# Weight preparation cut into paced steps, and routing steps moved, in a fused attention, mixture-of-experts and bilinear kernel

## The chip, the core and the metric

The kernel runs on one core of a Trainium2 chip. Five engines take part, each working through its own instructions in their order: TensorE (PE, with weight loads listed apart as PEld), VectorE (DVE), ScalarE (ACT), GpSimd (POOL), and SyncE (SP), which issues nearly all DMA. They meet only at semaphores. The metric is the device time of one execution in microseconds, taken as the median of several runs; lower is better.

## The reference

Three stages follow one another on 2304 tokens (4 sequences of 576) of width 512.

```python
# 1. linear attention, 8 heads of 64; phi gives 2 x 128 features
q_p, k_p = phi(q), phi(k)
kv  = einsum('bhsf,bhsd->bhfd', k_p, v);  z = k_p.sum(axis=2)
num = einsum('bhsf,bhfd->bhsd', q_p, kv)
den = einsum('bhsf,bhf->bhs', q_p, z)[..., None] + 1e-06
x = num / den                                  # becomes 2304 x 512
# 2. mixture of experts, 8 experts, one expert per token
logits = x @ w_gate + modality_bias[modality_id]
e_idx = argmax(logits, 1); gate_w = softmax(logits)[row, e_idx]
out[mask] = gate_w[mask, None] * (relu(x[mask] @ w1[e]) @ w2[e])     # 512 -> 1024 -> 512
# 3. bilinear layer, d_ff = 1536
return (out @ w_a) * (out @ w_b) @ w_out
```

All inputs of the first two stages are float32. The three weights of stage 3 arrive as float64 (8 bytes a number) and are narrowed to float32 on the chip.

## The kernel before

**Numbers in two parts.** Most matmuls of stages 2 and 3 work on operands that are split into a rounded high part and the remainder, and make three products (helper lines L54, L55, L56: high by high, low by high, high by low). ACT casts the high part and DVE subtracts to get the low one. Such pairs are `wh`/`wl` (expert weights, L552/L553), `mxh`/`mxl` (gathered tokens, L576/L577), `hh`/`hl` (the hidden layer, ACT L591 and DVE L592) and `yh`/`yl` (the input of stage 3, L747/L748, with differences `ysum` made first at L762).

**Attention** runs in rounds over units of two heads or so: `pjp` projections (PE) to `m` and `df` (DVE) to `kp` (ACT), then `kxp` (PE), its copy `kx` (DVE, L217), `qtp` transposes (PE) copied to `qts` (ACT, L190), `nmp` (PE), and `rec` and `x` (DVE). PE's order there is the order in which the code issues. Tokens are treated in two halves of 1152; each half has a route.

**Routing** of a half turns its logits into an expert and a place for each token: a gate (`lg`, `mx`, `gt`), a rank, a place (`vals`, `col`, `pl`) and a table. The table is two lookups by one-hot matmuls: `tbp` gives `idx`, the tokens of each tile, and `tbq` gives `perm` and `g2`, for the way back. The first half's steps are handed to attention's rounds 4, 5 and 7 and have a lower priority; the second half's go to slots of the expert stage.

**The expert stage** has 4 tiles of tokens and 8 slots per tile. A slot is 48 matmuls. In slots 0 to 3 the loop `l1` makes two of the eight blocks of the hidden layer: PE fills `hp`, ACT makes `hh`, DVE makes `hl`, and two blocks are under way at most before PE needs the first one's buffer back. In slots 4 to 7 `l2` makes one of four output blocks in two groups of columns; ACT copies each group from `yp` to `y` (L604). At the start of a slot the code runs that slot's entries of a table `side`, then splits the weights of two slots on, and in slots 4 to 6 transposes the next tile's gathered tokens (`mxt`, L573).

**Weight preparation for stage 3** is such side work. The 1536 columns are 12 blocks `f`; ten are prepared during the expert stage, two in stage 3. For each half block `narrow` fetches the raw 8-byte numbers (SP, L688, 768 KB), ACT takes the absolute value (`cvs`, L692), POOL clamps from below (L693), and DVE builds the float32 numbers (L694, L696, L698, L699, L701). After both halves DVE forms sums of the parts (L710 to L713, each 128x256), ACT and DVE split the result (`whi`, L718; `wsum`, L719) in two ranges of 1024 and 1280 columns, and SP stores both parts to a scratch `wsc` (L720, L721). In stage 3 `fw` is loaded from there (L730).

**Order.** Instructions of each engine are put in order by a planner that follows priorities and its own estimates of time. The ten preparations are given a priority lower by 200 than the rest, each as one block of work issued at a slot spread from 3 to 28 of 32. At slot 28 `open_first` closes the preparation's buffers, opens the pools of stage 3 in the same place (so that `ysum` may lie where a `wsum` was), issues the first loads of `fw`, and prepares the first tokens of stage 3 (`first`: two differences, five casts `yh`, five remainders `yl`), at the low priority too.

**The branch.** After the last slot stands `If(nts > NTMIN)` (L983): more tiles only for an uneven routing. It is not taken with these inputs. In the program, PE's first matmul behind it waits for ACT's and DVE's counts that cover everything ahead of the branch on these two engines.

**Stage 3** makes 504 groups of `abp` from `yh`/`yl` and `fw`, multiplies, and multiplies by the third weight; results leave by an indirect DMA of POOL.

Of the kernel before, what the change touches and what calls it, by code (L numbers as in the profile page):

```python
# [20 lines left out]
P = 128  # L21
# [37 lines left out]
class Attn:  # L59
    def __init__(self, nc, tc, ctx, cst, qk, v, vt, xs, lgp):  # L60
        self.nc, self.tc = nc, tc
        self.qk, self.v, self.vt, self.xs = qk, v, vt, xs
        self.cst, self.lgp = cst, lgp
        pool = lambda n, b, **kw: ctx.enter_context(tc.tile_pool(name=n, bufs=b, **kw))
        self.p_ld = pool("a_ld", 2, side="right")
        self.p_df = pool("a_df", 5, side="right")
        self.p_v = pool("a_v", 3)
        self.p_x = pool("a_x", 2)
        self.p_sm = pool("a_sm", 4)
        self.p_kx = pool("a_kx", 2)  # L70
# [130 lines left out]
    def kx(self, u, b):  # L201
# [11 lines left out]
        x = st["kx", b] = self.p_kx.tile([P, 2, 2, 73], F32, tag=f"kx{b}", name="kx")  # L213
        if u == 1 and not b:
            self.first = nc.vector.tensor_copy(x, ps).ins
        else:
            nc.vector.tensor_copy(x, ps)  # L217

    def num(self, u, *parts):
# [4 lines left out]
        for b, h in parts:  # L224
            qt = st.pop(("qt", b, h))
            for j in range(4 if b < 2 else 2):
                for c in range(2):
                    for m in range(2):
                        mm = slice(64 * m, 64 * m + 64)
                        kx = st["kx", b if b < 2 else m][:, c, h if b < 2 else j, :]  # L230
                        nc.tensor.matmul(ps[mm, o, :], qt[:, c, j, mm], kx, start=c == 0, stop=c == 1)
# [102 lines left out]
class Route:  # L334
# [4 lines left out]
    def steps(self, wk, ps, tag, after=None):  # L339
# [7 lines left out]
        return [start, self.rank, self.place, self.table]  # L347
# [4 lines left out]
    def gate(self):  # L352
# [10 lines left out]
        for m in range(2):  # L363
# [3 lines left out]
            nc.vector.tensor_add(lg, lg if m else self.lgp, tmp)  # L367
        mx = self.w([NG], "mx")
        nc.vector.tensor_reduce(out=mx, in_=lg, op=ALU.max, axis=AX.X)
        nc.vector.tensor_sub(lg, lg, mx.unsqueeze(2).to_broadcast([P, NG, E]))  # L370
        ex = self.w([NG, E], "ex")
# [24 lines left out]
    def place(self):  # L396
# [12 lines left out]
        sel = self.w([NG, E], "sel")  # L409
        vals = self.w([3, NG], "vals")  # L410
        for i, src in enumerate((R[:, :NG, :], pf[:, 0, :].unsqueeze(1).to_broadcast([P, NG, E]),
                                 pf[:, 1, :].unsqueeze(1).to_broadcast([P, NG, E]))):
            nc.vector.tensor_mul(sel, oh[:, :NG, :], src)
            nc.vector.tensor_reduce(out=vals[:, i, :], in_=sel, op=ALU.add, axis=AX.X)
        r, te, of = vals[:, 0, :], vals[:, 1, :], vals[:, 2, :]

        def floordiv(val, steps, name):
            k = steps.shape[1]
            t = self.w([NG, k], name + "c")
            nc.vector.tensor_tensor(out=t, in0=val.unsqueeze(2).to_broadcast([P, NG, k]),  # L420
                                    in1=steps.unsqueeze(1).to_broadcast([P, NG, k]), op=ALU.is_ge)
            q = self.w([NG], name + "q")
            nc.vector.tensor_reduce(out=q, in_=t, op=ALU.add, axis=AX.X)
            return q

        def rest(val, q, step, name):
            t = self.w([NG], name)
            nc.vector.scalar_tensor_tensor(out=t, in0=q, scalar=-float(step), in1=val, op0=ALU.mult, op1=ALU.add)
            return t

        jt = floordiv(r, c["kts"][:, 1:KMAX], "jt")
        rc = rest(r, jt, TS, "rc")
        jb = floordiv(rc, c["kp"][:, 1:NSUB], "jb")
        self.pl = rest(rc, jb, P, "pl")
        col = self.col = self.w([NG], "col")
        nc.vector.tensor_add(col, te, jt)
        nc.vector.scalar_tensor_tensor(out=col, in0=col, scalar=float(NSUB), in1=jb, op0=ALU.mult, op1=ALU.add)
        pc = self.w([NG], "pc")
        nc.vector.tensor_add(pc, of, r)
        self.cq = floordiv(pc, c["kp"][:, 1:NG], "cq")  # L440
        self.cl = rest(pc, self.cq, P, "cl")
# [23 lines left out]

    def table(self):
        nc, c = self.nc, self.cst
        NC = NTMAX * NSUB
# [7 lines left out]

        def onehot(out, i, v, n):
            if not self.bp:
                for g in range(NG):
                    nc.gpsimd.tensor_scalar(out=out[:, g, :], in0=c[i][:, :n], scalar1=v[:, g:g + 1], scalar2=None,  # L480
                                            op0=ALU.is_equal)
                return
            nc.vector.tensor_tensor(out=out, in0=c[i][:, :n].unsqueeze(1).to_broadcast([P, NG, n]),
                                    in1=v.unsqueeze(2).to_broadcast([P, NG, n]), op=ALU.is_equal)

        def lookup(name, col, n, row, parts):
            k = len(parts)
            hot = self.w([NG, n], name + "h", BF16)
            rhs = self.w([NG, k, n], name + "r", BF16)
            lhs = self.w([NG, P], "lhs" if self.bp else name + "l", BF16)  # L490
            onehot(hot, "icol", col, n)
            for i, v in enumerate(parts):
                (nc.vector if self.bp else nc.gpsimd).tensor_mul(rhs[:, :, i, :], hot, v.unsqueeze(2).to_broadcast([P, NG, n]))
            onehot(lhs, "i128", row, P)
            ps = self.ps.tile([P, 512], F32, tag=self.tag, name=name)
            for g in range(NG):
                nc.tensor.matmul(ps[:, :k * n], lhs[:, g, :], rhs[:, g].rearrange("p a n -> p (a n)"),
                                 start=g == 0, stop=g == NG - 1)
            return [ps[:, i * n:(i + 1) * n] for i in range(k)]

        def token(out, hi, lo, base):
            t = self.w([NC], "tk")[:, :hi.shape[1]]
            nc.vector.tensor_scalar(out=t, in0=hi, scalar1=float(1 << TB), scalar2=float(base), op0=ALU.mult, op1=ALU.add)
            nc.vector.tensor_add(out, t, lo)

        toks = [c["tokp"][:, i, :] for i in range(2)]
        self.idx = self.pool.tile([P, NC], I32, name=f"idx{self.bp}")
        self.g2 = self.pool.tile([P, NG], F32, name=f"g2{self.bp}")
        self.perm = self.pool.tile([P, NG], I32, name=f"perm{self.bp}")
        hi, lo = lookup("tbp", self.col, NC, self.pl, toks)  # L510
        token(self.idx, hi, lo, 0)
        hi, lo, *gs = lookup("tbq", self.cq, NG, self.cl, toks + [gp[:, i, :] for i in range(3)])
        token(self.perm, hi, lo, HALF * self.bp)
# [6 lines left out]
class Moe:  # L520
# [26 lines left out]
    def splitw(self, T, j):  # L547
# [5 lines left out]
        nc.vector.tensor_sub(lo, src, f32(hi))  # L553
# [25 lines left out]
    def l1(self, T, f):  # L579
# [11 lines left out]
        nc.scalar.activation(hh, ps[:, :, :CG], AF.Relu)  # L591
        nc.vector.scalar_tensor_tensor(out=hl, in0=ps[:, :, :CG], scalar=0.0, in1=f32(hh), op0=ALU.max,  # L592
                                       op1=ALU.subtract)
        T["h", f] = (hh, hl)

    def l2(self, T, m):
        nc = self.nc
        wh, wl = T["w", 4 + m]
        for g in range(2):
# [57 lines left out]
class Moe2:  # L657
# [14 lines left out]
    def pools(self, ctx, ps_a, ps_l):  # L672
# [3 lines left out]
        self.p_t[1] = pool("f_t1", 4)  # L676
# [4 lines left out]
    def narrow(self, pool, f, half, dst, nt):  # L681
        nc = self.nc
        n = 768
        if not self.f64:
            nc.sync.dma_start(out=dst, in_=self.w[f][:, n * half:n * half + n])
            return
        raw = pool.tile([P, n, 2], I32, tag="raw", name="raw", bufs=2)
        nc.sync.dma_start(out=raw.rearrange("p n w -> p (n w)"), in_=self.w[f][:, 2 * n * half:2 * n * half + 2 * n])  # L688
        lo, hi = raw[:, :, 0], raw[:, :, 1]
        t = pool.tile([P, n], I32, tag="t", name="cvt", bufs=nt)  # L690
        s = pool.tile([P, n], I32, tag="s", name="cvs", bufs=nt)
        nc.scalar.activation(s.bitcast(F32), hi.bitcast(F32), AF.Abs)  # L692
        nc.gpsimd.tensor_scalar(out=s.bitcast(F32), in0=s.bitcast(F32), scalar1=LEAST, scalar2=None, op0=ALU.max)  # L693
# [9 lines left out]
    def prep(self, f, pool, nw, nt):  # L703
        nc = self.nc
        w = pool.tile([P, 2304], F32, tag="w", name="wsum", bufs=nw)
        for half, c in enumerate((0, 1280)):
            self.narrow(pool, f, half, w[:, c:c + 768], nt)
# [6 lines left out]
        for x, y in self.CUTS:  # L714
# [6 lines left out]
            nc.sync.dma_start(out=self.wsc[f][1][:, x:y], in_=src)  # L721

# [169 lines left out]
def trn_kernel(ctx, tc, qk, v, vt, w_phi, mod_id, w_gate, bias, wm, wf, out):  # L892
# [10 lines left out]
    with ExitStack() as actx:  # L903
# [13 lines left out]
        for r in range(9):  # L917
            if r + 1 < 8:
                at.load(r + 1)
            if r == 2:  # L920
                bs = bias_load(nc, cpool, keep, bias, mod_id)
                routes = [Route(tc, rpool, lgp[i], bs[i], i) for i in range(2)]
                rsteps = [low(tc, st) for st in routes[0].steps(wkpool, at.ps_c, "c", at.first)]
# [3 lines left out]
            at.round(r, {4: {2: rsteps[:1]}, 5: {2: rsteps[1:3]}, 7: {0: rsteps[3:]}}.get(r, {}) if r > 2 else {})  # L927
            if r == 8:
                order.close()
    with ExitStack() as mctx:  # L930
# [24 lines left out]
        side = {k: [low(tc, rs[f])] for f, k in enumerate((0, 2, 4, 8))}  # L955
# [99 lines left out]
```

## Time and profile before

| | us |
|---|---|
| median of 3 runs (lowest, highest) | 829.94 (828.87, 830.32) |
| the profiled execution, its own time | 837.45 |
| its span, first to last instruction | 835.7 |
| attention, to the first expert matmul | about 176 |
| expert stage, to its last matmul | 176 to 409 |
| stage 3 | 410 to 836 |

The mean granted TensorE clock in the profiled execution is 0.991 of full speed. In the rows further down, a row of a timeline is: start in us, duration in us, engine and line, operation, output and inputs, shape, and in square brackets the idle time that the engine had just before and what released it. A row of waits is: engine, output and line waited for by it, the releaser, then total us, times, longest us. A row of windows is: the stretch in us, its length, then busy us and instruction counts of PE, PEld, DVE, ACT, POOL, then the granted clock, the DMA share and GB/s. A release by `ACTq L983` means the branch at line 983 on ACT's sequencer.

### The profile page before, as it was taken

The numbers are of one execution on the slowest core, as the hardware profiler recorded it, in microseconds if no ns is written. First come the engines' busy times: TensorE is split into PE (matmuls) and PEld (weight loads), VectorE is DVE, ScalarE is ACT, GpSimd is POOL, SyncE is SP. The second block draws the span as 40 slices with busy tenths as digits, with TensorE's granted clock in tenths as the row PEclk, the third lists the DMA queues.
The fourth block names the chain that finished last, engine by engine and source line by source line (L and its number), as shares of the span: only waits on it lengthen the run. The fifth ranks groups of instructions, "written<-read, shape, count | busy, mean of one in ns | idle before, by whom it ended". The sixth has DMA issues, their size and how long they took to land.

```text
span 835.7 us, 18329 instructions
## 1 busy us (share of the span) xinstructions
PE 804.0 (96%) x7283; PEld 755.5 (90%) x7284; DVE 595.1 (71%) x1071; ACT 373.8 (45%) x665; POOL 140.4 (17%) x164
## 2 busy tenths in 40 slices
PE   8999999889999999979999999999999999999996
PEld 6999888789999999979999899999999999999995
DVE  5888898589998999987488854775544676445553
ACT  3656555344544455453345433553333364333332
POOL 1000009342217433310021100030000002000002
PEclk9999999999999999999999999999999999999998
DMA  7666432466768888776499776576666568665632
GB/s 272 193 183 195 149 120 82 115 206 225 249 238 300 289 302 296 271 240 266 170 360 339 254 281 207 187 271 226 205 206 201 186 223 280 206 198 189 224 123 92
DMA packets 85163, 184.22 MB, mean 220 GB/s; under 512 B 27760, under 2 KB 37520, under 8 KB 85072
## 3 DMA queue, kind: packets, MB, share of 16 engines
q1 hardware_dynamic: 81872, 173.21, 61.4%
q0 software_dynamic: 3040, 9.72, 3.4%
q8 instruction: 58, 0.95, 0.5%
q14 instruction: 33, 0.27, 0.1%
q10 hardware_dynamic: 160, 0.07, 0.0%
HBM read 145.21 MB, written 37.75 MB: 219 GB/s over the span
## 4 chain that ended last, share of the span: by engine, by line
issue 44%; PE 4%; POOL 3%; POOLq 0%; ACT 0%
POOL out L800 2%; PE abp L54 1%; PE abp L56 1%; PE abp L55 1%; POOL cvs L693 1%; PE op L55 0%; PE op L54 0%; PE op L56 0%; POOLq L1052 0%; ACT cvs L692 0%; POOLq L800 0%; ACT pc L844 0%
## 5 line engine op out<-in xcount | busy, mean ns | idle before, releaser
L844 ACT COPY pc<-abp 128x384 f32<-128x384 f32 x252 | 120.6, 479 | 199.6 <-PE abp L56 195.9
L54 PE MATMUL abp<-yh,fw 128*128 128x384 f32 x504 | 170.1, 337 | 2.4 <-ACT pc L844 1.3
L56 PE MATMUL abp<-yh,fw 128*128 128x384 f32 x504 | 170.0, 337 | 0.0
L55 PE MATMUL abp<-yl,fw 128*128 128x384 f32 x504 | 169.8, 337 | 0.0
L54 PEld LDWEIGHTS abp<-yh,fw 128*128 128x128 f32 x504 | 94.6, 188 | 11.6 <-ACT pc L844 2.4
L55 PEld LDWEIGHTS abp<-yl,fw 128*128 128x128 f32 x504 | 94.7, 188 | 7.4
L693 POOL TENSOR_SCALAR cvs<-cvs 128x768 f32<-128x768 f32 x24 | 61.5, 2562 | 198.1 <-ACT cvs L692 184.4
L56 PEld LDWEIGHTS abp<-yh,fw 128*128 128x128 f32 x504 | 94.6, 188 | 0.0
L54 PE MATMUL hp<-mxh,wh 128*128 128x304 f32 x256 | 79.1, 309 | 7.9 <-DVE hl L592 6.8
L55 PE MATMUL op<-fw,gh 128*128 128x512 f32 x216 | 85.7, 397 | 0.0
L54 PE MATMUL op<-fw,gh 128*128 128x512 f32 x216 | 85.1, 394 | 0.0
L56 PE MATMUL op<-fw,gl 128*128 128x512 f32 x216 | 85.0, 394 | 0.0
L55 PE MATMUL yp<-hl,wh 128*128 128x304 f32 x256 | 77.3, 302 | 1.7 <-DVE hl L592 1.7
L55 PE MATMUL hp<-mxl,wh 128*128 128x304 f32 x256 | 78.2, 306 | 0.0
L56 PE MATMUL hp<-mxh,wl 128*128 128x304 f32 x256 | 77.8, 305 | 0.0
L56 PE MATMUL yp<-hh,wl 128*128 128x304 f32 x256 | 77.8, 304 | 0.0
L54 PE MATMUL yp<-hh,wh 128*128 128x304 f32 x256 | 76.9, 302 | 0.0
L800 POOL DMA_INDIRECT out<-o,perm x18 | 18.3, 1019 | 348.3 <-ACT o L799 341.2
L190 ACT ACTIVATE qts<-qtp 128x512 f32<-128x512 f32 (+1 forms) x80 | 38.3, 558 | 64.8 <-PE qtp L187 64.8
L855 DVE TENSOR_TENSOR d<-u,pc 128x768 f32<-128x768 f32 x36 | 34.5, 957 | 32.2 <-ACT pc L844 32.0
L54 PEld LDWEIGHTS hp<-mxh,wh 128*128 128x128 f32 x256 | 48.7, 190 | 9.4 <-issue 6.4
L156 DVE TENSOR_REDUCE m<-pjp 128x8 f32<-128x1024 f32 (+2 forms) x49 | 45.1, 933 | 12.0 <-PE pjp L154 12.0
(191 smaller groups left out, 1587.5 us busy)
## 6 DMA issues: line engine op xcount, KB each, us to landing
fw<-wsc SPq DMA_DIRECT2D x72, 512.0 KB, 5.4
fw<-wsc SPq DMA_DIRECT2D x144, 256.0 KB, 3.3
raw<-in_moe_w SPq DMA_DIRECT2D x24, 768.0 KB, 7.2
s<-in_moe_w SPq DMA_DIRECT2D x32, 512.0 KB, 4.2
fw<-wsc SPq DMA_DIRECT2D x72, 128.0 KB, 5.7
wsc<-whi SPq DMA_DIRECT2D x12, 640.0 KB, 4.3
wsc<-wsum SPq DMA_DIRECT2D x12, 640.0 KB, 6.8
wsc<-whi SPq DMA_DIRECT2D x12, 512.0 KB, 7.0
```

The lines of the kernel that those rows point to most:

```text
L54: nc.tensor.matmul(out, lh, rh, start=start, stop=False)
L55: nc.tensor.matmul(out, lh, rl, start=False, stop=False)
L56: return nc.tensor.matmul(out, ll, rh, start=False, stop=stop).ins
L156: nc.vector.tensor_reduce(out=mv, in_=pv, op=ALU.max, axis=AX.X, apply_absolute_value=True)
L190: nc.scalar.activation(t[:, s, :n, :], ps[:, :n, :], AF.Exp, scale=1.0 - 2.0 * s)
L693: nc.gpsimd.tensor_scalar(out=s.bitcast(F32), in0=s.bitcast(F32), scalar1=LEAST, scalar2=None, op0=ALU.max)
L800: st = nc.gpsimd.indirect_dma_start(out=self.out[:, :], out_offset=bass.IndirectOffsetOnAxis(ap=self.routes[bp].perm[:, c:c + 1], axis=0), ...
L844: copied = nc.scalar.copy(x, ps).ins
L855: nc.vector.tensor_add(d, u, x.unsqueeze(1).to_broadcast([P, 2, n]))
```

## The change

There are five parts.

1. Two pools of attention, `a_df` and `a_ld`, change places, so that the expert stage's buffers lie over other tiles of attention.
2. Routing is cut into seven steps instead of four: the gate into start and score, the place into place and bounds, the table into `table` (`tbp`) and `back` (`tbq`, `perm`, `g2`). The first half's steps go to rounds 4, 5, 5, 6, 7 and 8; the second half's to slots 0, 0, 2, 4, 4, 8, 8.
3. The transposes of the first expert tile from the third on, and the second weight split, are issued only behind the last copy of `kx` (and from the fourth on behind the last `nmp` matmul).
4. A preparation is cut into fetch, clamp (ACT and POOL) and narrow (DVE, with sums and stores in the second half). The 20 half blocks get slots of their own from 2 on; fetch, clamp and narrow of one go to slots k, k+1 and k+2, each issued only behind the latest `hh`/`y` instruction of ACT and the latest `wl`/`hl` instruction of DVE. Three raw buffers instead of two.
5. In stage 3 the last two preparations are cut in the same way, and one pool of `y` tiles has 3 buffers instead of 4.

```diff
+        self.p_df = pool("a_df", 5, side="right")
         self.p_ld = pool("a_ld", 2, side="right")
-        self.p_df = pool("a_df", 5, side="right")
...
-        return [start, self.rank, self.place, self.table]
+        return [start, self.score, self.rank, self.place, self.bounds, self.table, self.back]
...
+    def run(self, tiles, side={}, at=None):
...
+        behind = lambda i, on: self.tc.issue_after(i) if at and on else nullcontext()
         split(0)
         for j in range(NSUB):
-            self.transp(Ts[0], j)
+            with behind(at and at.copied, j > 1), behind(at and at.last, j > 2):
+                self.transp(Ts[0], j)
...
-        split(1)
+        with behind(at and at.copied, True):
+            split(1)
...
-        self.p_t[1] = pool("f_t1", 4)
+        self.p_t[1] = pool("f_t1", 3)
...
+    def jobs(self, f, pool, nw, nraw, ns):
+        st = {}
+
+        def fetch(half):
+            st["raw", half] = self.fetch(f, half, pool, nraw)
+
+        def clamp(half):
+            st["s", half] = self.clamp(st["raw", half], pool, ns)
+
+        def narrow(half):
+            if not half:
+                st["w"] = self.sumw(pool, nw)
+            self.narrow(f, half, st["raw", half], st["s", half], pool, st["w"])
+            if half:
+                self.park(f, st["w"], pool)
+
+        return fetch, clamp, narrow
...
-                rsteps = [low(tc, st) for st in routes[0].steps(wkpool, at.ps_c, "c", at.first)]
+                rsteps = routes[0].steps(wkpool, at.ps_c, "c", at.first)
+                rsteps = [low(tc, st) for st in rsteps[:6] + [lambda: routes[0].back(at.ps_q, "q")]]
...
-            at.round(r, {4: {2: rsteps[:1]}, 5: {2: rsteps[1:3]}, 7: {0: rsteps[3:]}}.get(r, {}) if r > 2 else {})
+            at.round(r, {4: {2: rsteps[:1]}, 5: {0: rsteps[1:2], 2: rsteps[2:4]}, 6: {2: rsteps[4:5]}, 7: {0: rsteps[5:6]},
+                         8: {0: rsteps[6:]}}.get(r, {}) if r > 2 else {})
...
-        def conv(f):
-            with tc.high_priority(offset=-LOWP):
-                m2.prep(f, cv[0], 2, 2)
-
-        K0, K1 = 3, len(tiles) * mo.NJ - 4
+        def conv(f, half, job):
+            def run():
+                with tc.high_priority(offset=-LOWP), tc.issue_after(mo.act), tc.issue_after(mo.dve):
+                    job(half)
+            return run
+
+        K0, K1 = 2, len(tiles) * mo.NJ - 4
         for f in range(NPRE):
-            side.setdefault(K0 + (K1 - K0) * f // NPRE, []).append(lambda f=f: conv(f))
+            fetch, clamp, narrow = m2.jobs(f, cv[0], 2, 3, 2)
+            for half in range(2):
+                k = K0 + (K1 - 2 - K0) * (2 * f + half) // (2 * NPRE)
+                for i, job in enumerate((fetch, clamp, narrow)):
+                    side.setdefault(k + i, []).append(conv(f, half, job))
```

How it moves instructions is seen at three places. In the changed kernel the lines have other numbers (`hl` L603, `wl` L564, `cvt` L720 and L722, `cvs` L724 and L725, `wsum` L727 and L745, sums L736 to L739, `whi` L744, `y` L615, `yh` L791, `yl` L792, `ysum` L806).

First, VectorE at the end of attention, before: the rows of the two lookups (`tk`, `idx0` from `tbp`; `tk`, `perm0`, `g20` from `tbq`) and the next unit's `m`.

```order
L504 TENSOR_TENSOR idx0_2633<-tk_2669,tbp_2659 128x45
L503 TENSOR_SCALAR tk_2708<-tbq_2698 128x9
L504 TENSOR_TENSOR perm0_2635<-tk_2708,tbq_2698 128x9
L514 COPY g20_2634<-tbq_2698 128x9
L515 TENSOR_TENSOR g20_2634<-g20_2634,tbq_2698 128x9
L516 TENSOR_TENSOR g20_2634<-g20_2634,tbq_2698 128x9
L517 TENSOR_TENSOR g20_2634<-g20_2634 128x9
L156 TENSOR_REDUCE m_2715<-pjp_2717 128x8
```

Now, on the same engine, the place where `tbq` is read, at the start of the expert stage.

```order
L588 TENSOR_TENSOR mxl_3144<-mxt_3159,mxh_3143 128x4x128
L564 TENSOR_TENSOR wl_3181<-s_3135,wh_3180 128x1024
L502 TENSOR_SCALAR tk_2978<-tbq_2968 128x9
L316 TENSOR_TENSOR m8_3202<-w8_3190 128x64
L319 TENSOR_SCALAR ltri_3204<-i128_3186,part_3200 128x128
L329 TENSOR_SCALAR tokp0_3214<-tok_3208 128x9
L329 TENSOR_SCALAR tokp1_3217<-tok_3208 128x9
L237 TENSOR_SCALAR rec_3002<-nmp_2985 128x4
L503 TENSOR_TENSOR perm0_2941<-tk_2978,tbq_2968 128x9
L525 COPY g20_2940<-tbq_2968 128x9
```

The second lookup's work has moved by two rounds, behind the third `mxl`, between the constants of the second route and the last `rec` and `x`.

Second, VectorE in the first slots of the last expert tile, before: from the third block's `hl` (`hl_5546`) to the next two.

```order
L592 SCALAR_TENSOR_TENSOR hl_5546<-hp_5520,hh_5545 128x608
L699 SCALAR_TENSOR_TENSOR cvs_5481<-raw_5478,cvs_5481 128x768
L713 TENSOR_TENSOR wsum_5318<-wsum_5318 128x256
L694 TENSOR_SCALAR cvt_5491<-cvs_5492 128x768
L701 TENSOR_TENSOR wsum_5477<-cvt_5480,cvs_5481 128x768
L719 TENSOR_TENSOR wsum_5318<-wsum_5318,whi_5345 128x1024
L553 TENSOR_TENSOR wl_5579<-s_5417,wh_5578 128x1024
L696 SCALAR_TENSOR_TENSOR cvt_5491<-raw_5489,cvt_5491 128x768
L592 SCALAR_TENSOR_TENSOR hl_5575<-hp_5549,hh_5574 128x608
L592 SCALAR_TENSOR_TENSOR hl_5610<-hp_5584,hh_5609 128x608
```

Now, from the third block's `hl` (`hl_5530`) to the next two.

```order
L603 SCALAR_TENSOR_TENSOR hl_5530<-hp_5504,hh_5529 128x608
L737 TENSOR_TENSOR wsum_5079<-wsum_5079 128x256
L738 TENSOR_TENSOR wsum_5079<-wsum_5079 128x256
L722 SCALAR_TENSOR_TENSOR cvt_5330<-raw_5158,cvt_5330 128x768
L739 TENSOR_TENSOR wsum_5079<-wsum_5079 128x256
L724 TENSOR_SCALAR cvs_5252<-cvt_5330 128x768
L745 TENSOR_TENSOR wsum_5079<-wsum_5079,whi_5242 128x1024
L725 SCALAR_TENSOR_TENSOR cvs_5252<-raw_5158,cvs_5252 128x768
L564 TENSOR_TENSOR wl_5583<-s_5428,wh_5582 128x1024
L603 SCALAR_TENSOR_TENSOR hl_5559<-hp_5533,hh_5558 128x608
L727 TENSOR_TENSOR wsum_5329<-cvt_5330,cvs_5252 128x768
L603 SCALAR_TENSOR_TENSOR hl_5614<-hp_5588,hh_5613 128x608
```

Between the third and the fourth `hl` stood six rows of preparation and a `wl`, and now seven and a `wl`. The row that reads a freshly clamped `cvs` (`cvt_5491<-cvs_5492` before) stands there no more; its like (`cvt_5330<-cvs_5252`) has moved ahead of `hl_5530`, and its clamp was issued a slot before.

Third, ScalarE at the end of the expert stage, ahead of the branch, before: copies to `y` with the casts `yh`.

```order
L604 COPY y1_3068<-yp_5814 128x304
L747 CAST yh_5732<-y0_3067 128x768
L604 ISA
L604 COPY y1_3068<-yp_5840 128x304
L747 CAST yh_5736<-ysum_5730 128x768
L747 CAST yh_5740<-y0_3067 128x768
L747 CAST yh_5746<-ysum_5744 128x768
L747 CAST yh_5750<-ysum_5728 128x768
L604 ISA
L604 COPY y1_3068<-yp_5866 128x304
L604 ISA
L604 COPY y1_3068<-yp_5892 128x304
```

Now:

```order
L615 ISA
L615 COPY y1_3070<-yp_5896 128x304
L615 ISA
L615 COPY y1_3070<-yp_5922 128x304
L744 CAST whi_5577<-wsum_5488 128x1280
L615 ISA
L615 COPY y1_3070<-yp_5948 128x304
L791 CAST yh_5736<-y0_3069 128x768
L791 CAST yh_5740<-ysum_5734 128x768
L791 CAST yh_5744<-y0_3069 128x768
L791 CAST yh_5750<-ysum_5748 128x768
L791 CAST yh_5754<-ysum_5732 128x768
```

The five `yh` casts have moved behind the last copy to `y`, and the last `whi` cast of 1280 columns now stands between the last two copies.

## Rows read from the trace of the kernel before

**Rows 1.** The page's first lines: busy time by engine.
```profile
PE 804.0 (96%) x7283; PEld 755.5 (90%) x7284; DVE 595.1 (71%) x1071; ACT 373.8 (45%) x665; POOL 140.4 (17%) x164
```

**Rows 2.** What PE waited for, over the whole span.
```profile
PE hp L54 <- DVE hl L592: 6.8, 4, 3.6
...
PE mxt L573 <- DVE mxl L577: 1.9, 1, 1.9
PE yp L55 <- DVE hl L592: 1.7, 1, 1.7
...
PE abp L54 <- ACT pc L844: 1.3, 3, 0.8
...
PE abp L54 <- ACTq L983: 1.0, 1, 1.0
```

**Rows 3.** What all engines waited for, one row of DVE.
```profile
DVE cvt L694 <- POOL cvs L693: 12.8, 6, 3.6
```

**Rows 4.** Timeline of DVE ahead of PE's longest idle time.
```profile
365.93 0.41 DVE L713 TENSOR_TENSOR wsum<-wsum 128x256 f32<-128x256 f32 x1
368.79 0.56 DVE L694 TENSOR_SCALAR cvt<-cvs 128x768 int32<-128x768 int32 x1 [2.45 <-POOL cvs L693]
...
370.14 1.22 DVE L719 TENSOR_TENSOR wsum<-wsum,whi 128x1024 fp32r<-128x1024 f32 x1
371.27 1.21 DVE L553 TENSOR_TENSOR wl<-s,wh 128x1024 fp32r<-128x1024 f32 x1
372.41 0.95 DVE L696 SCALAR_TENSOR_TENSOR cvt<-raw,cvt 128x768 int32<-128x768 int32 x1
373.28 1.48 DVE L592 SCALAR_TENSOR_TENSOR hl<-hp,hh 128x608 fp32r<-128x608 f32 x2
```

**Rows 5.** Timeline of PE, the matmul behind that idle time.
```profile
374.20 0.59 PE L54 MATMUL hp<-mxh,wh 128*128 128x304 f32 x1 [3.58 <-DVE hl L592]
```

**Rows 6.** Windows around it, with the granted clock.
```profile
374.00:376.00 2.00, 1.79 (x7) 1.83 (x8) 2.00 (x3) 0.17 (x1) 0.00 (x0) 0.50 0.70 204
376.00:378.00 2.00, 2.00 (x13) 2.00 (x12) 2.00 (x4) 0.00 (x0) 0.00 (x0) 0.72 1.05 433
```

**Rows 7.** DMA issues: queue, size, count, KB each, median us to landing.
```profile
raw<-in_moe_w SPq DMA_DIRECT2D x24, 768.0 KB, 7.2
...
wsc<-wsum SPq DMA_DIRECT2D x12, 640.0 KB, 6.8
```

**Rows 8.** Timeline of ACT at the end of the expert stage.
```profile
387.60 1.26 ACT L718 CAST whi<-wsum 128x1280 fp32r<-128x1280 f32 x1 [2.70 <-DMA wsc<-whi]
...
392.84 0.83 ACT L747 CAST yh<-y 128x768 fp32r<-128x768 f32 x1
...
405.89 0.41 ACT L604 COPY y<-yp 128x304 f32 x1 [2.89 <-PE yp L56]
409.27 0.41 ACT L604 COPY y<-yp 128x304 f32 x1 [2.96 <-PEq L983]
```

**Rows 9.** Timeline of DVE in the same stretch.
```profile
388.89 1.49 DVE L719 TENSOR_TENSOR wsum<-wsum,whi 128x1280 fp32r<-128x1280 f32 x1 [2.08 <-ACT whi L718]
...
394.58 0.95 DVE L762 TENSOR_TENSOR ysum<-y,ysum 128x768 f32<-128x768 f32 x1
...
398.83 1.82 DVE L748 TENSOR_TENSOR yl<-ysum,yh 128x768 fp32r<-128x768 f32 x2
410.18 0.96 DVE L762 TENSOR_TENSOR ysum<-y,ysum 128x768 f32<-128x768 f32 x1 [9.53 <-ACTq L983]
```

**Rows 10.** Timeline of PE, the first matmul of stage 3.
```profile
410.20 0.44 PE L54 MATMUL abp<-yh,fw 128*128 128x384 f32 x1 [1.02 <-ACTq L983]
```

**Rows 11.** Timeline of SP's DMA queue in the same stretch.
```profile
388.89 0.32 SPq L720 DMA_DIRECT2D wsc<-whi  x1
...
391.84 22.00 SPq L730 DMA_DIRECT2D fw<-wsc  x16
```

**Rows 12.** PE's lines from 140 to 155 us: the second lookup.
```profile
L497 PE MATMUL tbq<-tbqr,tbql 128*128 128x45 bf16 x9 | 0.4, 182 | 0.8 <-POOL tbqr L493 0.8
```

More of the change, by code (lines that the diff above doesn't have):

```diff
@@ L408, in place @@
             nc.vector.tensor_reduce(out=pf[:, i, :], in_=big, op=ALU.add, axis=AX.X)
[L409 to L434, printed above, removed]
+        self.tv, self.pf, self.vals = tv, pf, self.w([3, NG], "vals")
+        r = self.pick(0, R[:, :NG, :])
+        te = self.pick(1, pf[:, 0, :].unsqueeze(1).to_broadcast([P, NG, E]))
+        jt = self.floordiv(r, c["kts"][:, 1:KMAX], "jt")
+        rc = self.over(r, jt, TS, "rc")
+        jb = self.floordiv(rc, c["kp"][:, 1:NSUB], "jb")
+        self.pl = self.over(rc, jb, P, "pl")
         col = self.col = self.w([NG], "col")
@@ L486, in lookup @@
[L486 to L499, printed above, removed]
@@ L511, in table @@
-        token(self.idx, hi, lo, 0)
-        hi, lo, *gs = lookup("tbq", self.cq, NG, self.cl, toks + [gp[:, i, :] for i in range(3)])
-        token(self.perm, hi, lo, HALF * self.bp)
+        hi, lo, *gs = self.lookup("tbq", self.cq, NG, self.cl, self.toks + [gp[:, i, :] for i in range(3)], ps, tag)
+        self.token(self.perm, hi, lo, HALF * self.bp)
         nc.vector.tensor_copy(self.g2, gs[2])
@@ L679, in pools, with fetch, clamp, narrow @@
         self.ps_a, self.ps_l = ps_a, ps_l
[L681 to L683 removed]
+    def fetch(self, f, half, pool, n):
+        if not self.f64:
+            return None
+        c = 768 * 2
+        raw = pool.tile([P, 768, 2], I32, tag="raw", name="raw", bufs=n)
+        self.nc.sync.dma_start(out=raw.rearrange("p n w -> p (n w)"), in_=self.w[f][:, c * half:c * half + c])
+        return raw
+    def clamp(self, raw, pool, n):
+        if not self.f64:
+            return None
+        nc = self.nc
+        s = pool.tile([P, 768], I32, tag="s", name="cvs", bufs=n)
+        nc.scalar.activation(s.bitcast(F32), raw[:, :, 1].bitcast(F32), AF.Abs)
+        nc.gpsimd.tensor_scalar(out=s.bitcast(F32), in0=s.bitcast(F32), scalar1=LEAST, scalar2=None, op0=ALU.max)
+        return s
+    def narrow(self, f, half, raw, s, pool, w):
+        nc = self.nc
+        dst = w[:, 1280 * half:1280 * half + 768]
         if not self.f64:
[L685 removed]
+            nc.sync.dma_start(out=dst, in_=self.w[f][:, 768 * half:768 * half + 768])
             return
[L687 to L688 removed]
         lo, hi = raw[:, :, 0], raw[:, :, 1]
[L690 to L693, printed above, removed]
+        t = pool.tile([P, 768], I32, tag="t", name="cvt")
         nc.vector.tensor_scalar(out=t, in0=s, scalar1=3, scalar2=0x3FFFFFF8,
@@ L701, in narrow, with sumw, park @@
         nc.vector.tensor_add(dst, t.bitcast(F32), s.bitcast(F32))
-    def prep(self, f, pool, nw, nt):
+    def sumw(self, pool, nw):
+        return pool.tile([P, 2304], F32, tag="w", name="wsum", bufs=nw)
+    def park(self, f, w, pool):
         nc = self.nc
-        w = pool.tile([P, 2304], F32, tag="w", name="wsum", bufs=nw)
-        for half, c in enumerate((0, 1280)):
-            self.narrow(pool, f, half, w[:, c:c + 768], nt)
         a11, a12, a21, s2, s1, a22 = (w[:, 256 * i:256 * i + 256] for i in range(6))
```

111 lines of the change are left out of this document (77 added, 34 removed).

## The prediction, made before the changed kernel was run

> **What bounds the kernel now.** I read the busy times first: PE is at work for 96% of the span [rows 1], and DVE is next with 71%. The span is therefore PE's own work plus its idle time, and a change that leaves the matmuls alone, as this one does, can act only on the idle time and on the clock at which PE restarts. Next I read PE's waits [rows 2]. In the expert stage PE waits for DVE's `hl`: 6.8 us in four places in front of `hp` and 1.7 us in one place in front of `yp`, 8.5 us in all. It waits 1.0 us at the branch. Nothing else in the list that the change touches is over 2 us.
>
> Why is `hl` late? DVE works in order, and preparation rows stand in front of `hl`. Among the waits of all engines DVE's `cvt` waits for POOL's clamp, 12.8 us in six places [rows 3]. The longest of PE's gaps shows the mechanism [rows 4, 5]: DVE sits for 2.45 us until 368.79 because `cvt` wants a clamp that isn't done, then works through five preparation or weight rows, and the overdue `hl` pair starts at 373.28. PE restarts at 374.20 after 3.58 us idle. The two windows behind it read a granted clock of 0.50 and 0.72 [rows 6], the first at the lower level of 1.2 GHz: 2 x 0.50 + 2 x 0.28 = 1.6 us of matmul time lost on top. The gap and its echo cost 5.2 us.
>
> **Part 4, the paced preparation: what it removes.** In the old order one block of work fetched, clamped and used its data, so DVE reached `cvt` while the fetch and the clamp were still on their way. A fetch takes 7.2 us to land [rows 7], a slot is two groups of 3.38 us (the two last copies of `y` start at 405.89 and 409.27 [rows 8]), so 6.8 us. With fetch, clamp and narrow in three successive slots, `cvt` follows its fetch by about 13.5 us, 7.2 of which the transfer takes; the clamp on POOL has the rest. The waits on POOL should go.
>
> What is late next is DVE's own work. Between `hl_5530` and `hl_5559` stand eight rows: three sums of 0.41, L722 0.95, L724 0.56 (as the row of `cvt` that has its size), L745 1.22, L725 0.95, `wl` 1.21, together 6.1 us, or 5.4 us from start to start since neighbours overlap by 0.09 (370.14 to 371.27 for a row of 1.22 [rows 4]). With `hl` itself, 0.7, DVE needs 6.2 us where a block takes 3.4, so the fourth `hl` starts 2.8 us late. PE feels it only when `hl` of block f is not done as block f+2 begins: 3.38 - 0.78 - 0.14 (end of the first `hl` at 374.06, restart at 374.20) = 2.5 us. Counted through all 32 blocks in the same way, six come out at 2.1 to 2.8 us late, and the rest below. So the cover is used up in six places, and any short wait on top of it (`wl` for `wh`, a clamp behind other work of ACT) becomes PE idle time. Bounds for what is left of the 8.5 us: 0.3 us (DVE alone) and 8.5 us (the stalls come back in other places). I take 1.5 us, near the lower end, since the row that named POOL carries 12.8 us and its reason is removed. Gain: 8.5 - 1.5 = 7.0 us, and the 1.6 us of clock, 8.6 us.
>
> **The same part at the branch: what it adds.** The 20 half blocks now run to the last slots, and the order of ACT shows the price: the `whi` cast of 1280 columns of the last block stands between the last two copies to `y`, and the five casts `yh` stand behind the last one. DVE's tail hangs on them: `wsum`, two `ysum`, `yl`, `ysum`, and four `yl`. In the program PE's first `abp` waits for ACT's and DVE's counts of everything ahead of the branch. The trace of before can't show the price, as DVE had ended at 400.65 (398.83 + 1.82) and stood idle for 9.53 us [rows 9], and PE lost only 1.02 us, from 409.18 to 410.20 [rows 10], 0.52 us behind ACT's last copy (409.27 + 0.41).
>
> I put the new order on the old times, with 409.18 as the end of PE's expert work:
> - The next to last copy ends at 406.30; `whi` 1.26 us [rows 8], to 407.5; DVE's `wsum` 1.49 us [rows 9], to 409.0.
> - Its store of 640 KB follows. The second `ysum` is written where this `wsum` lay and waits for the store. Nearest row: a store of that size was issued at 388.89 and the next load, which waits for stores, went at 391.84 [rows 11], 2.95 us later. The median to landing of all twelve such stores is 6.8 us [rows 7], most of them among other traffic. Bounds: no wait, and 6.8 us. I take 3.0 us, as nothing but stores is moving there: landed at 412.1.
> - The second `ysum` (0.95) ends at 413.0, the first `yl` 0.95 at 413.9 (its `yh` is done by 410.5), the `ysum` at 414.8, its `yh` (0.83) at 415.6, its `yl` at 416.5, and three more `yl` at 0.87 to 0.91 at 419.2.
> - With 0.52 us at the branch PE restarts at 419.7: idle for 10.5 us where it was 1.02, so 9.5 us more. Without the wait for the store it would be 417.5, 7.3 us more; with 6.8 us to land, 13.3 us more.
>
> Behind such a gap PE restarts at the lower clock, as it did at 374.20; I charge the same 1.6 us [rows 6], and take no more for a longer gap. In all 11.1 us. The first `fw` loads need the stores too; they lie beside this chain, and would cost the excess if they landed after 419.7.
>
> The page "DMA: Bandwidth & Descriptors" of the Trainium skill (section "Anatomy of one DMA") gives a transfer a constant of about 2.0 us plus its bytes at 436 GB/s, for DMAs issued by GpSimd; as an estimate by it, 640 KB take 3.5 us. The row of 2.95 us is shorter and the median of 6.8 us longer, so the rule stands between them, and by it the restart would be half a microsecond later and the sum 832.3.
>
> **Parts 1 to 3, attention and routing.** The second lookup leaves the place where PE waited 0.8 us for POOL and then spent 0.4 us on nine matmuls [rows 12]. The matmuls are done elsewhere at the same price; the wait can go whole, or the next thing (`pjp`, held back by `df`) can take its place. Six small DVE rows of `tbq` now stand among the first `mxl`, where PE already waits 1.9 us [rows 2]; that is worth up to some tenths against it. Bounds: a gain of 0.8, and a loss of 1.9 if that wait doubles. I take a gain of 0.6, since the lookup is off PE's path in the new place. The second half's finer steps (slots 0 to 8) are small DVE rows in tile 0, where the counting above finds no block later than 1.5 us: nothing. The swap of the pools lets two `mxh` casts come earlier: counted in the 0.6.
>
> **Part 5, stage 3.** Two preparations in paced steps and a pool of 3 instead of 4: PE's waits there sum to 1.3 us in three places, for ACT's `pc` [rows 2]. Nothing, with 0.5 either way.
>
> **Sum.** + 9.5 + 1.6 at the branch, - 7.0 - 1.6 in the expert stage, - 0.6 in attention: + 1.9 us. Against the profiled execution's 837.45 us (span 835.7) that is 839.3 (837.6). The profiled execution is 7.5 us above the median of 829.94; I carry the difference over unchanged, so 831.8 us.
>
> **The rivals.**
> - *The join is cheaper than the gains.* DVE has no wait for the store (7.3 instead of 9.5), the residue is 0.3, attention gives 0.8: + 7.3 + 1.6 - 8.2 - 1.6 - 0.8 = - 1.7, 828.2 us. For it: the store may have landed by the time, if `whi` runs ahead. Against: `whi` can't run ahead of the copy in front of it on ACT.
> - *PE doesn't wait for the whole tail* but only for its first operands `yh`, `yl`: done at 413.9, restart at 414.4, 4.2 us more instead of 9.5: 826.5 us, and 821 if the tail ran earlier altogether. Against: the counts in the program; before, PE restarted behind ACT's last copy, of which its first matmul needs nothing.
> - *The paced steps only move the stalls.* The change doesn't do what it says: DVE's cover is used up in six blocks, a wait for `wh` or a clamp of about 1 us in each gives back 5 us, and one drop of clock 1.6 more. Then + 11.1 - 2 - 0.6 = + 8.5, 838.4 us. It decides from about 1 us of wait on those six `hl`. Against: the fetch has a slot more than before.
> - *The store is slow* (6.8 us, as the median): 3.8 us more than the forecast, 835.6 us, and the first `fw` loads with it. It decides if `fw` loads or fetches run beside the store.
>
> **How the numbers follow.** Forecast, 829.5 to 834.5 us, chance 0.50; the join cheaper, 0.18; PE waits for the first operands only, 0.08; stalls only moved, 0.12; the store slow, 0.12. A difference below 0.2%, 1.66 us, is about what a measurement of this kernel can't tell from none: faster is below 828.3, slower above 831.6. Slower: 0.25 of the forecast's 0.50, and 0.24 from the last two, 0.49. No change: 0.22 of the forecast and 0.06 of the first rival, 0.28. Faster: 0.03 + 0.12 + 0.08 = 0.23. The range of 8 in 10 is 826.5 to 837.
>
> **What would show it.** In the profile of the changed kernel: DVE's wait of `cvt` for POOL gone or below 2 us; PE's waits for `hl` at 1 to 2 us in all; between the last `yp` and the first `abp` about 10 us of PE idle time, ACT's `yh` casts and DVE's `yl` in it, and a clock near 0.5 behind it; `tbq` without its 0.8 us. The prediction is wrong if PE goes on within 3 us of its last `yp`, or if its waits for `hl` are still 5 us.

## The result, and the profile after

The changed kernel takes 834.62 us in the median of 6 runs (832.08 to 836.67), the kernel before 829.82 us beside it: a ratio of 1.0055, 95% interval 1.0028 to 1.0081. On a second chip the same two gave 1.0107 (1.0070 to 1.0144). It is slower on both, by 4.8 us between the first pair of medians.

The profiled execution says less at first sight: 834.70 us with a span of 832.9 us, shorter than the 835.7 us of before. The execution shown of before was 7.5 us above its median, with gaps in attention that the changed kernel's doesn't have, so the spans can't be set against each other; stages can. First, what PE waits for in the changed kernel (columns as in [rows 2]):

```profile
PE abp L54 <- DVEq L1037: 12.2, 1, 12.2
PE abp L54 <- ACT pc L888: 3.4, 3, 2.9
PE hp L54 <- DVE x L242: 1.5, 1, 1.5
...
PE nmp L231 <- DVE kx L214: 1.0, 1, 1.0
```

The rows of `hl`, 8.5 us before, are gone altogether, and so is that of `tbq`. In DVE's waits the 12.8 us of `cvt` for POOL's clamp [rows 3] have no row any more either. The 1.0 us at the branch has become 12.2 us. Busy time of the expert stage in one window each, before and then after (columns as in [rows 6]):

```profile
173.00:409.00 236.00, 226.32 (x1629) 223.33 (x1627) 203.55 (x334) 110.06 (x155) 74.10 (x34) 0.99 0.73 256
```

```profile
163.00:388.00 225.00, 223.48 (x1627) 221.98 (x1626) 202.55 (x325) 109.03 (x151) 67.24 (x34) 1.00 0.72 253
```

The stage is 10.8 us shorter (173.16 to 409.18 before, where the table of before says about 176 for its start; 163.09 to 388.33 now), and PE is idle for 1.5 us of it. The end of the stage on ACT, DVE and PE shows what was paid:

```profile
385.36 1.27 ACT L744 CAST whi<-wsum 128x1280 fp32r<-128x1280 f32 x1
388.43 0.41 ACT L615 COPY y<-yp 128x304 f32 x1 [1.80 <-PEq L1037]
388.74 0.83 ACT L791 CAST yh<-y 128x768 fp32r<-128x768 f32 x1
395.75 0.83 ACT L791 CAST yh<-ysum 128x768 fp32r<-128x768 f32 x1 [6.18 <-DVE ysum L806]
...
413.84 0.89 ACT L708 ACTIVATE cvs<-raw 128x768 f32<-128x768 f32 x1 [2.74 <-DMA raw<-in_moe_w]
```

```profile
386.66 1.49 DVE L745 TENSOR_TENSOR wsum<-wsum,whi 128x1280 fp32r<-128x1280 f32 x1 [4.20 <-ACT whi L744]
...
393.02 0.96 DVE L806 TENSOR_TENSOR ysum<-y 128x768 f32<-128x768 f32 x1 [4.00 <-DMA wsc<-wsum]
...
398.36 1.82 DVE L792 TENSOR_TENSOR yl<-ysum,yh 128x768 fp32r<-128x768 f32 x2
```

```profile
400.49 0.66 PE L54 MATMUL abp<-yh,fw 128*128 128x384 f32 x1 [12.16 <-DVEq L1037]
415.56 0.45 PE L54 MATMUL abp<-yh,fw 128*128 128x384 f32 x1 [2.88 <-ACT pc L888]
```

This is the chain of the prediction, row for row: `whi` between the last two copies, `wsum`, a `ysum` that waits for the store, then `yh` and `yl`, with the last `yl` done at 400.18 and PE on its way at 400.49. Where [rows 9] show DVE idle for 9.53 us, it is now the one that is waited for. The second PE row was not foreseen: 12 us after the restart PE stops again, for 2.88 us, since ACT stands at a `cvs` whose raw data isn't there. Behind it in ACT's order are `pc`, the copies that take finished `abp` groups out of PE's way, and `gh`, a cast of their product. Before, the same `cvs` stood behind two `gh` and its data came in time:

```profile
419.58 0.51 ACT L831 CAST gh<-ca 128x384 fp32r<-128x384 f32 x1
420.05 0.48 ACT L844 COPY pc<-abp 128x384 f32<-128x384 f32 x1
420.42 0.91 ACT L692 ACTIVATE cvs<-raw 128x768 f32<-128x768 f32 x1
```

SP's queue says why the raw data is late, and the windows what both gaps do to the clock:

```profile
388.18 0.32 SPq L747 DMA_DIRECT2D wsc<-wsum  x1
393.02 13.99 SPq L774 DMA_DIRECT2D fw<-wsc  x16
407.05 1.43 SPq L700 DMA_DIRECT2D raw<-in_moe_w  x2
```

The fetch is queued behind 16 loads of `fw`. The first eight wait for the store: 4.84 us from 388.18 to 393.02. The row of x16 hides a second wait, which narrower views show:

```profile
393.02 3.72 SPq L774 DMA_DIRECT2D fw<-wsc  x8
403.35 3.66 SPq L774 DMA_DIRECT2D fw<-wsc  x8
```

```profile
SPq L1037 <- SPq L1037: 6.0, 4, 4.0
SPq L774 <- DMA wsc<-wsum: 4.3, 1, 4.3
```

SP meets the branch too, behind its first eight loads, and waits there for 6.0 us. The profile doesn't name what for; these loads had landed when it went on, as nothing moves any more in the window of 402 to 404 below (0 GB/s). Only at 403.35 do the next eight go, and behind them the fetch, 6.6 us after PE's restart where it was 3.7 us before (413.88 against 410.20).

```profile
402.00:404.00 2.00, 2.00 (x8) 2.00 (x7) 0.00 (x0) 1.17 (x2) 0.00 (x0) 0.50 0.00 0
404.00:406.00 2.00, 2.00 (x8) 2.00 (x7) 1.57 (x3) 1.25 (x3) 0.00 (x0) 0.50 0.71 227
...
416.00:418.00 2.00, 2.00 (x9) 1.80 (x8) 1.62 (x5) 1.61 (x3) 1.72 (x2) 0.56 1.01 394
418.00:420.00 2.00, 2.00 (x8) 1.90 (x7) 1.97 (x3) 0.00 (x0) 1.51 (x1) 0.59 0.73 252
```

PE runs at the lower clock until about 406, and again from 416 to 420: from the restart on, busy time times the missing share of the clock is 2.8 and 1.7 us. From the first `abp` to the end, stage 3 takes 432.4 us where it took 425.5 (835.7 - 410.20).

### The profile page after: what moved, and what is told of

Read it like the earlier page. It is cut to its first block, busy times and chain, and to the rows that moved or that the text cites. A ratio compares the mean times of both kernels' runs of the same rounds, so it can differ in the third digit from the quotient of the medians.

```text
span 832.9 us, 18335 instructions
## 1 busy us (share of the span) xinstructions
PE 801.8 (96%) x7283; PEld 754.7 (91%) x7284; DVE 600.9 (72%) x1071; ACT 376.0 (45%) x665; POOL 135.9 (16%) x164
## 4 chain that ended last, share of the span: by engine, by line
PE 32%; issue 16%; ACT 1%; DMA 1%; DVE 1%; POOL 0%; SPq 0%; POOLq 0%; DVEq 0%; ACTq 0%
PE abp L54 7%; PE abp L56 7%; PE abp L55 7%; PE op L56 4%; PE op L55 4%; PE op L54 4%; DMA raw<-in_moe_w 1%; ACT pc L888 0%; POOL out L844 0%; SPq L774 0%; DVE gl L876 0%; ACT gh L875 0%; DVE ca L874 0%; ACT yh L791 0%; DVE o L841 0%
## 5 line engine op out<-in xcount | busy, mean ns | idle before, releaser
L54 PE MATMUL abp<-yh,fw 128*128 128x384 f32 x504 | 171.9, 341 | 15.5 <-DVEq L1037 12.2
L54 PEld LDWEIGHTS abp<-yh,fw 128*128 128x128 f32 x504 | 95.7, 190 | 25.3 <-issue 12.4
L56 PEld LDWEIGHTS abp<-yh,fw 128*128 128x128 f32 x504 | 95.7, 190 | 0.0
L876 DVE TENSOR_TENSOR gl<-ca,gh 128x384 fp32r<-128x384 f32 x72 | 39.8, 558 | 19.0 <-ACT gh L875 15.6
```

The costliest lines, as they stand in the source:

```text
L54: nc.tensor.matmul(out, lh, rh, start=start, stop=False)
L56: return nc.tensor.matmul(out, ll, rh, start=False, stop=stop).ins
L876: nc.vector.tensor_sub(gl, ca[:, i, :], f32(gh))
```

## The experiments

Ratios are to the kernel before, on the same chip, with 95% intervals. `attn`, `pace`, `npre9` and `fsfirst` shared one chip, `after_again`, `late`, `fslate` and `noif` another, the last four a third; profiles are compared by stage, because the gaps named `issue` come and go with the chip (see `before_again`).

**attn.** The new attention, routing and splits with the old preparation: `Moe2.narrow` and `prep`, the old `conv` and stage 3's old side entries put back.

```diff
-                    side.setdefault(k + i, []).append(conv(f, half, job))
+            side.setdefault(K0 + (K1 - K0) * f // NPRE, []).append(lambda f=f: conv(f))
```

> Parts 1 to 3 alone (pools, routing steps, splits behind the last copies), with the old block-wise preparation. The join theory (the loss lies at the branch and in what follows it, and comes from part 4): no late casts, PE idle at the branch about 1 us, waits for hl still about 8 us, time 827 to 829.5 us. The rival, that the moved routing steps and splits cost the time: 832 to 835 us, with new idle time of PE before the first expert matmul.

Ratio 0.9956 (0.9939 to 0.9974), 822.94 us beside 826.46. The branch costs 1.0 us again, and the waits for `hl` are about half:

```profile
PE hp L54 <- DVE hl L603: 3.3, 4, 1.2
...
PE yp L55 <- DVE hl L603: 1.3, 1, 1.3
PE abp L54 <- ACTq L1001: 1.0, 1, 1.0
```

Parts 1 to 3 help, by 3.6 us, and not by the 0.6 us of the prediction; the waits for `hl` were expected to stay at about 8 us and fell to 4.6.

**pace.** The other half: the paced preparation, with the pools, rounds and splits as before. (The finer slots for the second half's routing, of part 2, stay in both `attn` and `pace`.)

```diff
-            with behind(at and at.copied, j > 1), behind(at and at.last, j > 2):
-                self.transp(Ts[0], j)
+            self.transp(Ts[0], j)
```

> Parts 4 and 5 (paced preparation), with attention's pools, the first half's routing rounds and the splits as before. The join theory: waits for hl near 0, PE idle about 12 us at the branch, 832 to 836 us. The rival that parts 1 to 3 cost the time: 822 to 828 us.

Ratio 1.0100 (1.0072 to 1.0127), 834.73 us; no wait for `hl` is left, and the branch reads:

```profile
PE abp L54 <- DVEq L1032: 12.4, 1, 12.4
PE abp L54 <- ACT pc L885: 4.0, 5, 1.6
PE mxt L584 <- DVE mxl L588: 1.9, 1, 1.9
```

Behind the restart there are two shorter stops here, of 1.3 and 1.6 us, in place of the one of 2.9. So the loss comes with parts 4 and 5, and parts 1 to 3 take some of it back. The product, 1.0100 x 0.9956 = 1.0056, agrees with the first ratio of the change more closely than intervals of this width let one expect; the second chip gave 1.0107.

**npre9.** The changed kernel with 9 blocks in the expert stage, at the same pace, and 3 in stage 3. The five `yh` then stand ahead of the last two copies.

```diff
-NPRE = 10
+NPRE = 9
...
-                k = K0 + (K1 - 2 - K0) * (2 * f + half) // (2 * NPRE)
+                k = K0 + (K1 - 2 - K0) * (2 * f + half) // 20
```

> The changed kernel with 9 blocks prepared in the expert stage at the same pace, 3 in stage 3. The order then has the yh casts ahead of the last two copies to y. The join theory: PE idle at the branch at most 2 us, no half clock behind it, no 2.9 us wait for pc, waits for hl still near 0: 834.6 - 11 - 6 = 817.6 us, up to 821 if the third block costs something in stage 3. A rival, that stage 3's paced steps (part 5) cost the time whatever the branch does: 823 to 830 us with waits for pc of 3 us or more.

Ratio 0.9889 (0.9869 to 0.9908), 816.84 us beside 826.46: faster than both kernels. No row of `hl`, and:

```profile
PE abp L54 <- ACTq L1037: 1.0, 1, 1.0
...
PE abp L54 <- ACT pc L888: 0.8, 3, 0.3
```

One block less at the tail takes away the 11 us at the branch, the half clock behind it and the late fetch together. That stage 3's third block costs something shows nowhere: 425.1 us from its first `abp`, 425.5 before.

**fsfirst.** The pool of `ysum` laid over the raw buffers instead of the last `wsum`.

```diff
+            m2.p_s = ctx.enter_context(tc.tile_pool(name="f_s", bufs=1, **tl))
             m2.p_t[0] = ctx.enter_context(tc.tile_pool(name="f_t", bufs=Moe2.NT0, **tl))
-            m2.p_s = ctx.enter_context(tc.tile_pool(name="f_s", bufs=1, **tl))
```

> The changed kernel with the pool of ysum laid first, over the raw buffers and not over the last wsum, so that the store is waited for only by the second yl. If the 4.0 us for which ysum waited for the store lengthen the join as the prediction's chain has it: PE idle at the branch 12.2 - 3.5 = 8.7 us, time 831 us. If the join hangs on ACT's order alone: idle 12 us, 834.6 us.

Ratio 1.0126 (1.0104 to 1.0148), 836.38 us. The idle time at the branch fell as worked out, but the time did not:

```profile
397.37 0.66 PE L54 MATMUL abp<-yh,fw 128*128 128x384 f32 x1 [8.82 <-DVEq L1037]
415.57 0.69 PE L54 MATMUL abp<-yh,fw 128*128 128x384 f32 x1 [5.64 <-ACT pc L888]
```

PE restarts 3.1 us earlier than in the changed kernel, and stops again until 415.57, where the changed kernel had gone on at 415.56. With `cvs` where it is on ACT, the raw fetch and not PE's restart sets when the second column block may go: it was issued at 406.77 (407.05 in the changed kernel), since the store, the first loads and SP's wait at the branch ahead of it had hardly moved, and its `cvs` ran at 413.85 (413.84). What is saved at the first wait is paid at the second.

**after_again, late, noif** ran together, on another chip.

> The changed kernel once more, on the chip that the runs beside it use. Both theories: ratio to before 1.003 to 1.008 again; PE idle at the branch 12 us, then a wait for pc of about 3 us near 15 us after the restart.

Ratio 1.0107 (1.0070 to 1.0144), above the 1.003 to 1.008 expected, though the interval overlaps the first one. Branch 12.1 us, wait for `pc` 2.6 us: the same picture.

For **late** stage 3's two preparations are spaced wider:

```diff
-                side.setdefault(2 * (f - NPRE) + i, []).append(lambda job=job, half=half: job(half))
+                side.setdefault(3 * (f - NPRE) + (0, 2, 3)[i], []).append(lambda job=job, half=half: job(half))
```

> The changed kernel with stage 3's two preparations spaced wider: fetch in slot 0, clamp in slot 2, narrow in slot 3 (and 3, 5, 6 for the second block). Theory: the wait for pc (2.9 us) and the second fall of the clock (1.7 us) come from ACT's cvs, which stands ahead of pc and waits for a raw fetch that is queued behind the first fw loads. Both go: 4 to 5 us faster than the changed kernel on the same chip; the branch stays at 12 us. Rival, that the slow start of stage 3 comes from late fw loads: no difference, and PE waits for fw.

Ratio 1.0097 (1.0065 to 1.0129): nothing gained. This is a miss of the edit. A slot sets only when the code hands the work over; the planner put `cvs` in the same place on ACT, ahead of `gh`:

```profile
414.74 0.89 ACT L708 ACTIVATE cvs<-raw 128x768 f32<-128x768 f32 x1 [3.35 <-DMA raw<-in_moe_w]
415.53 0.50 ACT L875 CAST gh<-ca 128x384 fp32r<-128x384 f32 x1
```

**fslate**, the same spacing with `fsfirst`, came out no better:

> The wider spacing of stage 3 together with ysum laid over the raw buffers. If the 3.4 us saved at the branch by the second edit were only given back through the late raw fetch, they now stay: idle 8.8 us at the branch, no wait for pc, 3 to 4 us faster than the wider spacing alone. If they are given back through fw, as fast as the wider spacing alone.

Ratio 1.0123 (1.0090 to 1.0155), branch 8.2 us, wait for `pc` 5.6 us.

For **noif** the block under `If(nts > NTMIN)` is taken out.

> The changed kernel without the branch: the tiles of an uneven routing are left out of the program (they don't run with these inputs). The order on ACT is as before it. If the branch makes PE wait for the whole tail, PE now restarts behind the first yl: idle about 6.5 us. If the next chain behind it, the store and then the first fw load, ends at nearly the same time: idle 10 to 11.5 us, waiting for fw. If the branch had no part in it: 12 us, waiting for DVE.

Ratio 1.0146 (1.0103 to 1.0190). Without the branch PE doesn't wait for DVE's tail any more, but no less long, and longer than the 10 to 11.5 us expected:

```profile
PE abp L54 <- DMA fw<-wsc: 13.7, 1, 13.7
```

With the branch gone the planner issues the loads of `fw` in another order as well (from 386.82, around the last store), so the two numbers are not of one order. What holds is that the second chain, store and then `fw`, ends about when DVE's tail does (its last `yl` at 399.95, PE's restart at 400.67): taking out the branch alone gives no time back, ending the preparation earlier does (`npre9`).

**late2.** The clamps of stage 3 held on ACT behind the last `pc` of the second column block.

```diff
+                if i == 6:
+                    self.done = copied
...
+                with tc.issue_after(m2.done):
+                    job(half)
```

> The changed kernel with stage 3's clamps held on ACT behind the last pc copy of the second column block, so that no cvs stands ahead of the first block's gh and the second block's pc (the spacing alone had left it there). Theory: the wait for pc of 2.6 to 2.9 us and the second fall of the clock go, 4 to 5 us faster than the changed kernel's ratio of 1.0107: about 1.005. Rival, that late fw loads hold stage 3 back: PE waits for fw at the same place, ratio unchanged.

Ratio 1.0069 (1.0041 to 1.0096). The stop behind the restart is gone, and a shorter one stands further on:

```profile
404.64 0.66 PE L54 MATMUL abp<-yh,fw 128*128 128x384 f32 x1 [11.56 <-DVEq L1039]
453.99 0.44 PE L54 MATMUL abp<-yh,fw 128*128 128x384 f32 x1 [2.08 <-ACT pc L888]
```

```profile
451.89 1.26 ACT L744 CAST whi<-wsum 128x1280 fp32r<-128x1280 f32 x1 [2.49 <-DMA wsc<-whi]
```

There ACT is held by another row of the same kind, not by a clamp: a `whi` cast that waits for an earlier `whi` to be stored, again with `gh` and `pc` behind it, and the clock falls again (0.50 from 456 to 458). From first `abp` to first `op` (the product with the third weight) it takes 13.4 us, 16.6 in the changed kernel and 10.7 before. That `cvs` in front of `gh` and `pc` makes the first stop is shown; the 4 to 5 us expected are not, as a stop of 2.1 us took its place and the intervals of the ratios overlap.

**fslate2**, the held clamps with `fsfirst`:

> The same together with ysum laid over the raw buffers. If the 3.4 to 3.9 us saved at the branch are given back only through cvs: idle about 8.5 us at the branch, no wait for pc, 3 to 4 us faster than the held clamps alone. If the next fw loads take cvs's place: PE waits for fw in the first two column blocks and the gain over the held clamps alone is below 1 us.

Ratio 1.0026 (1.0003 to 1.0049), 0.43% or 3.6 us below `late2` on the same chip. With `cvs` out of the way the gain at the branch stays (the stop near 454 us isn't in this profile either, so not all of the 3.6 us need be the branch's), and the wait there has a new name:

```profile
404.30 0.66 PE L54 MATMUL abp<-yh,fw 128*128 128x384 f32 x1 [8.79 <-DMA fw<-wsc]
```

Three chains hang on the last store: DVE's tail (12 us at the branch), the loads of `fw` (9 us) and, for the second column block, the raw fetch behind SP's wait at the branch.

**attn9.** `attn` with 9 blocks at the old spacing (`NPRE = 9`, `// 10`).

> Parts 1 to 3 with the old block-wise preparation and 9 blocks in the expert stage. Rival to the paced steps: that the paced kernel with 9 blocks owes its gain only to the smaller work of DVE. Then this run is as fast, ratio 0.989. If pacing removes the waits for hl: some of them stay here (2 to 5 us), ratio 0.992 to 0.996.

Ratio 0.9920 (0.9891 to 0.9950). Some waits for `hl` stay:

```profile
PE hp L54 <- DVE hl L603: 2.8, 3, 1.4
...
PE yp L55 <- DVE hl L603: 1.3, 1, 1.3
```

So of the gain of `npre9` a good part comes from the new attention and the moved block, and pacing takes away the last 4.1 us of waits. In times that last step isn't shown: 0.9920 against 0.9889 on two chips, with intervals that overlap.

**before_again.**

> The kernel before once more, one look at its profile. If the gaps of issue at 148 to 152 us and the half clock behind them belong to that one execution: the first expert matmul at 168 to 170 us instead of 173, waits for hl again 8 to 9 us, PE idle at the branch 1.0 us, device time within 3 us of the median.

```profile
PE hp L54 <- DVE hl L592: 8.6, 7, 3.2
PE nmp L231 <- issue: 2.4, 5, 1.0
```

The waits for `hl` (8.6 and 1.7 us) and the branch (1.0) are there as before. The gaps of `issue` and the half clock behind them are there too, the first expert matmul is at 174.2, and the time, 840.04 us, lies 6.6 us above the median beside it, so my expectation missed: they are not of one execution. But `late2`, `fslate2` and `attn9` have the gaps as well on that chip (2.6 to 2.8 us; the half clock behind them only `fslate2`), and the changed kernel and the eight runs on other chips have 0.2 us or none in `nmp`. They belong to no part of the change, and a profile with them can't be set against one without.

## Why the prediction was right

It forecast 831.8 us, slower, with 826.5 to 837 as the range; 834.62 us lies in it, 2.8 us above the forecast and at the upper edge of the 829.5 to 834.5 us that had a chance of 0.50.

- **The waits for `hl`.** Gone as forecast, and more: 0 us left where 1.5 were allowed. The six blocks with no cover stayed on the safe side. The stage gained 10.8 us where 8.6 were forecast. It takes 225.2 us now and 224.8 us in `pace`, against 231.1 us in `attn`, so the pacing gets this without the new attention.
- **The branch.** The mechanism and its rows were right, the size a little small: 12.16 us idle, 10.5 forecast. The difference of 1.7 us is the store: `ysum` waited until 393.02, 4.84 us from its issue, where I took 3.0 us from [rows 11]; the bound of 6.8 us held. That is half of the way to the rival of the slow store.
- **The clock behind it.** 2.8 us lost, 1.6 charged. I took the price of a 3.6 us gap for one three times as long; the trace keeps 0.50 from the restart to about 406, so the term was mis-sized.
- **Stage 3, the term that failed.** "Nothing, with 0.5 either way" was wrong. The text had SP's queue in hand (the loads of `fw` wait for the stores) and asked only whether `fw` would be late, not what is queued behind `fw`, nor that SP has to pass the branch as well: the raw fetch came late, and ACT waits for it in order ahead of `gh` and `pc`. It cost 2.9 us and a second fall of the clock, 1.7 us; `late2` and `fsfirst` show it from both sides.
- **Attention.** Forecast 0.6 us, measured 3.6 us by `attn`, of which waits for `hl` (8.5 to 4.6 us between profiles) are a part that the planner's new order gave by the way. These waits alone fell by 3.9 us, more than the whole gain, so how much of the 3.6 us is attention's own isn't shown. Set against each other on two executions without `issue` gaps, `pace` and `attn` reach the first expert matmul at 168.1 and 163.7 us: 1.6 us of it at `tbq`, where the old place had stood in front of `pjp`, 0.7 us at `mxt`, whose wait of 1.9 us went, and 2.1 us ahead of 122 us, where the start of the two executions differs too (their first `pjp` behind the warm-up at 8.14 and 7.26). That last part stays open.

The two large terms were right in kind and nearly cancel, as forecast; what made it clearly slower is stage 3. That the total still lies near the forecast is in part luck. Costs that the sum lacked, 1.6 us at the branch, 1.2 us of clock and 4.6 us in stage 3, were partly paid by gains that it lacked: 2.2 us in the expert stage and, as what remains, an estimated 2.3 us in attention and elsewhere. The second chip's ratio, 1.0107, put on 829.82 us would be 838.7 us, above the range.

## What to carry to other kernels

Spreading side work evenly moves its end to the last moment, so look first at what waits for the last piece: here a branch, a store and two queues. When a wait is shortened and the time stays, look for the next chain that ends at the same place; here the tail, the loads and a fetch all hang on one late store, and moving that common cause, one block less in the stage, gave the time back. And follow an in-order queue to its end: a late load delays whatever is issued behind it, and whoever waits for that. The branch counts there too: here SP, which issues the loads, waited at it for 6.0 us.

## What was not expected of the hardware

- The last store of 640 KB, issued 1.5 us behind another of that size and ahead of any load, held its waiter for 4.84 us; 2.95 us were read from the trace of before. In `fsfirst`, `late`, `late2`, `fslate2` and `pace` the first load behind that store went 4.2 to 5.1 us after it. Why it takes longer than before stays open.
- The clock stayed at 0.50 for some 5.5 us behind a gap of 12.2 us in the changed kernel, and for about 3 us behind one of 3.6 us before [rows 6].
- Gaps of `issue` in `nmp` near 148 us, 2.4 to 2.8 us in all, show in the first profile of before and in all four kernels that shared the last chip, old and new, and in none of the nine profiles from elsewhere beyond 0.2 us.
